# Opening of an attention and Fourier-mixing kernel: heads' table on 128-row diagonals, four full products a query tile, and a new order of sums and scalings

## The chip, the cores and the metric

The kernel runs on one core of one Trainium2 chip. The metric is the device time of one execution in microseconds; the time before is the median of three runs. A profiled execution has a span of its own, from the first to the last instruction of the record, and the text keeps the two apart. Engines are named as the profile names them: PE is TensorE (PEld its weight loads), DVE is VectorE, ACT is ScalarE, POOL is GpSimd, SP is the queue that issues most DMAs.

## The reference

Efficient attention (two softmaxes and two small products), then a Fourier mixing layer with a layer norm and a feed-forward block. B = 8 batches, 8 heads of 64, S = 576 tokens, D = 512, all float32.

```python
q_s = softmax(q, axis=-1)                     # over the 64 columns of a head, + 1e-9 in the sum
k_s = softmax(k, axis=2)                      # over the 576 tokens, + 1e-9 in the sum
kv  = einsum('bhsd,bhse->bhde', k_s, v)       # one 64x64 table a head
x   = einsum('bhsd,bhde->bhse', q_s, kv)      # heads side by side: x is (B, 576, 512)
mixed = real(fft(fft(x, axis=1), axis=2))
u   = x + mixed
un  = (u - mean(u)) / sqrt(var(u) + 1e-6)     # over the 512 columns
out = u + maximum(un @ w_ch1, 0) @ w_ch2      # 512 -> 2048 -> 512
```

## The kernel before

All eight batches go through the same stages. Batch 0 is done alone in a hand-ordered opening, while the weights' first chunks load and are converted; from the first feed-forward products of batch 0 (`half`, L1467) a long script interleaves the feed-forward of one batch with the attention and mixing of the next.

**Order.** Steps are closures with a time. `opening` builds the steps of batch 0 and gives them names; the string `OPENING` lists name and time, and `WARM` lists filler products (`warm`, L270) whose results nobody reads. All steps of the kernel are sorted by that time, and each engine runs its own instructions in that order. The time is a sort key only; what an instruction waits for follows from the data and from the buffers.

**The opening, in the order of the data.** `first_keys` takes the keys of four head pairs (k00 to k03: 128 rows, two heads of 64, by 576 tokens): maximum on VectorE ("max", L554), exponential with its sum on ScalarE ("exp", L557), four transposes on TensorE ("turn", L562) and a copy out of PSUM on ScalarE ("four", L565). The fifth chunk of 64 tokens of all four is transposed together ("last", L570) and copied by VectorE ("fifth", L573). "inverse" (L576, L577) makes the reciprocals of the sums. "kv" (L586) multiplies keys and values into one PSUM tile, [128, 4, 64]: row 64h + d of pair r is row d of the table of head 2r + h. "scale" (L589) multiplies it by the reciprocals into `pairs[0]`, [128, 4, 65], whose 65th column holds ones and so gives the row sums of the queries.

The queries of batch 0 come as four tiles of 128 tokens: A (c = 0, u = 0), B (1, 1), C (0, 1), D (1, 0), and the shared tile t with the tokens that the folds treat apart. `q_exp_spread` is maximum (L968, VectorE), subtraction ("less", L973, GpSimd for A, B, C, VectorE for D and t) and exponential (L977, ScalarE). `q_turn` and `t_turn` transpose (L985) and copy (L996, L1006, ScalarE). The tile t is divided by its sums first (`q_inverse`, L946 to L957) and folded on GpSimd (`t_fold`, L1018 to L1026).

`own_times_kv` multiplies a tile by the table through `by_head` (L840): 4 pairs x 2 heads x 2 halves of the tokens, 16 products of 64 rows by 64 columns by 65, each on a quarter of the TensorE array. The profile counts two records of each float32 product, so 32. "inverse" (L862, L864) takes the reciprocal of the 65th column, "out" (L876) scales all 512 columns on VectorE; the same function can do it with eight activations on ScalarE, which `BY_ACT` chooses by tile. `t_times_kv` does the shared tile in the same way (L840 and L1061), ScalarE copies the results ("t parts", L1070 and L1073), and "t folds" (L1085 to L1088) folds them on VectorE.

`folded` adds and subtracts tokens: "tokens0" and "tokens2" are the sum and the difference of A and C, "tokens1" and "tokens3" those of D and B (L1104). "columns", "by" and "again" (L1110 to L1130) fold further, all on VectorE in batch 0. `blocks` holds the Fourier products: "e0" and "e1" (L1217) read the sums after "columns0" and "columns1", "e2" and "e3" (L1224) the differences, "tails" (L1234) reads the shared tile's folds. "z" and "y" copy the results out (L1246 to L1250; z2 and z3 on VectorE, the rest on ScalarE). `mix_own` (m0, m1: L1264 to L1295) transforms the columns, `norm` (L1321 to L1374) normalises and transposes for the feed-forward.

**Other work in these queues.** "roots" (L669) makes ScalarE load the table with the square root. "c0", "c1" and "c2" convert the first three chunks of weights (L391 to L399: two activations on ScalarE, two operations on VectorE, one addition on GpSimd). "kept0" (L632) keeps a copy of x of tile A in PSUM.

**Buffers.** PSUM tiles come from rings: `turned` (tag "tr", 2 buffers of one bank) and `two` (3 buffers of two banks). `flat` is `turned` seen as 512 columns. A new user of a buffer waits until the readers of the last one are done. `halves` gives the 512-column working tiles of the folds (6 buffers), the tag "root" a single small one.

## Time and profile before

| | |
|---|---|
| runs | 1005.66, 1006.8, 1005.86 us; median 1005.86 us |
| profiled execution, span | 1006.6 us |
| TensorE busy | 995.6 us, 99% |
| VectorE, ScalarE, GpSimd busy | 718.6, 493.2, 442.9 us |
| granted TensorE clock | full in each of the 40 slices |
| chain that ended last | PE 87%, DVE 7%, ACT 3%, DMA 1%, issue 1% |
| DMA | 236.37 MB, mean 235 GB/s |

The profile shows one execution. Rows of a timeline or of a chain have the start in us, the length in us, the engine, the line of the code and what is written and read; in brackets stands the idle time of the engine just before, and what ended it. "issue" is time in which the engine waited for nothing that the profile shows. Rows of the waits have the total in us, the number and the longest. A window row has, for a stretch, the busy time and the number of instructions of each engine, the granted clock (1.00 is full speed), the mean busy share of the DMA engines and their GB/s. Ends of matmuls are modelled, and starts of neighbours are the safer measure.

### The profile page before, as it was taken

To read this page: it belongs to the slowest core of one execution; us is meant where nothing else is said; L and a number is where in the kernel's file an instruction comes from. 1 tells how busy PE (TensorE), PEld (TensorE's weight loads), DVE (VectorE), ACT (ScalarE), POOL (GpSimd) and SP (SyncE) were. 2 spreads that over 40 slices of the span, in tenths; PEclk is the share of its full clock that TensorE was granted. 3 is DMA by queue.
4 is the path that set the end of the run, shared out by engine and by line. 5 is a ranking of instruction groups with operands and counts; after the bars stand their busy time and mean duration, and the time that the engine had idled before them with its cause. 6 is when DMAs were issued, how large, how long until landed. Compare 5 with 4: busy or idle time off the path is not lost.

```text
span 1006.6 us, 19808 instructions
## 1 busy us (share of the span) xinstructions
PE 995.6 (99%) x7562; PEld 855.7 (85%) x7562; DVE 718.6 (71%) x1356; ACT 493.2 (49%) x1277; POOL 442.9 (44%) x445
## 2 busy tenths in 40 slices
PE   8999999999999999999999999999999999999998
PEld 6844464888888899889988998899889998998897
DVE  6898898666765887588756877688667945685563
ACT  4585642872468228832775177625772342151200
POOL 4263420357535637664655465655646450040000
PEclk9999999999999999999999999999999999999999
DMA  9987499687989666975677577847753765674573
GB/s 300 258 281 245 158 240 346 205 243 226 342 283 272 230 230 219 266 237 210 251 220 242 206 269 237 253 174 270 231 204 135 267 213 200 224 265 172 183 256 132
DMA packets 123559, 236.37 MB, mean 235 GB/s; under 512 B 24184, under 2 KB 88440, under 8 KB 112840
## 3 DMA queue, kind: packets, MB, share of 16 engines
q1 hardware_dynamic: 123096, 234.58, 71.0%
q8 instruction: 60, 0.98, 0.4%
q14 instruction: 35, 0.29, 0.1%
q10 hardware_dynamic: 288, 0.26, 0.1%
q0 software_dynamic: 80, 0.26, 0.1%
HBM read 199.94 MB, written 39.06 MB: 237 GB/s over the span
## 4 chain that ended last, share of the span: by engine, by line
PE 87%; DVE 7%; ACT 3%; DMA 1%; issue 1%; SPq 0%; POOL 0%; DVEq 0%; POOLq 0%
PE bb L1544 16%; PE ba L1544 11%; PE bc L1544 11%; PE bb L1671 10%; PE ba L1671 7%; PE bc L1671 7%; PE bb L1641 5%; PE bc L1479 2%; PE bb L1760 2%; PE two L840 2%; PE one L755 2%; PE two L1207 1%; PE two L1264 1%; PE ba L1479 1%; PE bc L1760 1%; PE ba L1760 1%
## 5 line engine op out<-in xcount | busy, mean ns | idle before, releaser
L1544 PE MATMUL bb<-unT,big 128*128 128x256 f32 x768 | 183.3, 380 | 0.0
L1544 PEld LDWEIGHTS bb<-unT,big 128*128 128x128 f32 x768 | 144.8, 190 | 20.7 <-DVE u L1514 0.7
L1556 ACT ACTIVATE big<-big 128x512 f32<-128x512 f32 x96 | 59.8, 629 | 147.6 <-DVE big L1555 141.0
L1544 PE MATMUL ba<-unT,big 128*128 128x256 f32 x512 | 123.9, 382 | 0.0
L1544 PE MATMUL bc<-unT,big 128*128 128x256 f32 x512 | 121.5, 380 | 0.1
L817 ACT ACTIVATE qT<-q 32x128 f32<-32x128 f32 x384 | 117.9, 307 | 5.9 <-DVE q L807 0.8
L1544 PEld LDWEIGHTS bc<-unT,big 128*128 128x128 f32 x512 | 96.9, 190 | 13.7 <-DVE big L1555 0.5
L1544 PEld LDWEIGHTS ba<-unT,big 128*128 128x128 f32 x512 | 95.5, 190 | 13.9 <-issue 0.5
L1514 DVE TENSOR_TENSOR u<-bb,s 128x512 f32<-128x512 f32 x66 | 45.2, 685 | 85.0 <-PE bb L1544 66.5
L1671 PE MATMUL bb<-big 128*128 128x128 f32 x848 | 103.8, 276 | 0.2 <-DVE u L1678 0.2
L1671 PEld LDWEIGHTS bb<-big 128*128 128x128 f32 x848 | 98.9, 192 | 1.0 <-DVE u L1678 1.0
L1390 POOL COPY unT<-unT 32x256 f32<-32x256 f32 x98 | 42.0, 428 | 90.2 <-DVE unT L1382 85.9
L1621 POOL TENSOR_TENSOR x<-x,big 128x512 f32<-128x512 f32 x45 | 60.9, 1368 | 46.0 <-DVE big L1678 19.7
L1617 DVE TENSOR_TENSOR big<-big 128x512 f32<-128x512 f32 x98 | 79.9, 842 | 0.0
L1671 PE MATMUL ba<-big 128*128 128x128 f32 x640 | 79.0, 276 | 0.0
L1671 PEld LDWEIGHTS ba<-big 128*128 128x128 f32 x640 | 75.0, 192 | 0.8
L1390 ACT COPY unT<-unT 32x256 f32<-32x256 f32 x126 | 50.7, 402 | 31.3 <-DVE unT L1382 29.5
L804 POOL TENSOR_TENSOR q<-q,qm 128x512 f32<-128x512 f32 x24 | 25.8, 1073 | 88.2 <-DVE qm L799 53.1
L405 POOL TENSOR_TENSOR big<-big 128x512 f32<-128x512 f32 x24 | 30.4, 1268 | 68.4 <-ACT big L1556 68.4
L1641 PE MATMUL bb<-big 128*128 128x256 f32 x256 | 58.3, 379 | 0.0
L1555 DVE TENSOR_TENSOR big<-bc,u 128x512 f32<-128x512 f32 x64 | 44.0, 688 | 17.3 <-PE bc L1544 16.4
L1641 PEld LDWEIGHTS bb<-big 128*128 128x128 f32 x256 | 48.0, 190 | 6.1
(336 smaller groups left out, 1917.9 us busy)
## 6 DMA issues: line engine op xcount, KB each, us to landing
big<-w2d SPq DMA_DIRECT2D x67, 1024.0 KB, 4.6
big<-w1s SPq DMA_DIRECT2D x64, 896.0 KB, 4.7
big<-w2s SPq DMA_DIRECT2D x16, 1024.0 KB, 4.8
big<-in_w_dram SPq DMA_DIRECT2D x21, 512.0 KB, 6.0
w2d<-big SPq DMA_DIRECT2D x42, 256.0 KB, 6.5
kb<-in_kT_dram SPq DMA_DIRECT2D x28, 320.0 KB, 7.8
q<-in_q_dram SPq DMA_DIRECT2D x28, 256.0 KB, 6.0
vt<-in_v_dram SPq DMA_DIRECT2D x84, 80.0 KB, 2.7
```

Source lines behind the costliest of these rows:

```text
L405: e1.tensor_tensor(out=to(4), in0=at(2), in1=at(3), op=ALU.add)
L817: nc.scalar.activation(to[t, i * Q:i * Q + Q], one, ACT.Exp)
L1390: copy(to, of)
L1514: plus = lambda t: V.tensor_tensor(out=temp(t), in0=box["bb"][:], in1=box["s1"][:], op=ALU.add)
L1544: nc.tensor.matmul(bank()[:, i, :], lhsT=w[:, WA_AT[m], k * P:(k + 1) * P], rhs=self.unT[g][:, B_AT[m], k, :], start=first and i == 0 and ...
L1555: steps = [(0, lambda: V.tensor_tensor(out=hp(i), in0=bank()[:], in1=u()[:], op=ALU.add)), (0.8, lambda: nc.scalar.activation(hp(i), hp(i) ...
L1556: (0.8, lambda: nc.scalar.activation(hp(i), hp(i), ACT.Relu))]
L1617: e.tensor_tensor(out=to(o), in0=to(x), in1=to(y), op=op)
L1621: E.tensor_tensor(out=x, in0=x, in1=tile(m), op=ALU.add)
L1641: nc.tensor.matmul(box[name][:, i, :], lhsT=h[p][:, A_AT[m], i * P:(i + 1) * P], rhs=self.stream[n][:, p, :], start=p == 0 and (m != 1 or ...
L1671: nc.tensor.matmul(box[place[n]][:, i, :], lhsT=own(m)(A_AT[n])[:, f, :], rhs=w[:, r // 2, r % 2 * P:r % 2 * P + P], start=first and f == ...
L1760: nc.tensor.matmul(bank()[:, i, :], lhsT=h[p][:, A_AT[m], i * P:(i + 1) * P], rhs=w[:, p, :], start=first and i == 0 and p == 0, stop=p == ...
```

## The change

The heads' table of batch 0 moves from `pairs[0]` to a new tile `diagonal`, [128, 4, 2, 65], in a part of the weights' space that is still free. For pair r it holds 130 columns: head 2r in the upper 64 rows and the first 65 columns, head 2r + 1 in the lower 64 rows and the last 65, zeros elsewhere. The ones and zeros of the sum columns are set by four memsets on GpSimd; "inverse" multiplies them by the reciprocals (`both`), and "scale" multiplies the products by `both`, so that the zeros come out of the same operation. A query tile then needs four products of the full array, 128 rows by 128 tokens by 130 columns, instead of 16 (`first_times_kv`). The shared tile takes four products of 128 columns and four of 64 tokens by 128 columns, in two tiles of the "tr" ring (`first_t_times_kv`).

Moved between engines: the copy "fifth" from VectorE to ScalarE; "out" of tile B from VectorE to eight activations on ScalarE; "tokens2" from VectorE to GpSimd, behind a one-column copy (`gate`) that reads what "columns0" writes.

Moved in the order: "k0 inverse" ahead of A's maximum; C's and D's maxima behind B's; the turns of C, t and D behind the products of keys and values; "tokens0" and "columns0" between the scalings of C and B; "e0" ahead of the shared tile's product, "e1" behind it; "t folds" behind all other folds.

```diff
-8.90 A max, 9.50 B max, 9.58 k02 four, 9.65 A less, 9.77 k0 last, 10.10 k0 inverse, 10.27 k03 turn, 10.42 k0 fifth,
-10.69 B less, 10.80 A exp, 11.30 k03 four, 11.84 B exp, 11.85 A turn, 12.20 C max, 12.45 A copy, 12.80 D max, 12.90 C less,
-12.95 B turn, 13.00 t max, 13.10 D less, 13.20 t less, 13.55 B copy, 14.00 k00 kv, 14.01 k01 kv, 14.10 C exp, 14.11 C turn,
-14.12 D exp, 14.13 t exp, 14.14 C copy, 14.2 k02 kv, 14.3 k03 kv, 14.4 D turn, 14.41 D copy, 14.75 t inverse, 14.76 k0 scale,
-14.8 t normal, 15.0 A kv, 15.1 t turn, 15.31 t copy, 15.4 C kv, 15.45 B kv,
-18.48 A inverse, 18.50 A out, 18.60 C inverse, 18.61 C out, 18.62 D kv, 18.90 B inverse, 19.01 B out, 19.63 D inverse,
-19.70 D out, 20.00 t fold, 20.1 t join, 20.2 t kv, 20.3 t parts, 20.43 tokens0, 20.5 columns0, 20.6 e0,
-20.70 tokens1, 20.80 columns1, 20.9 e1, 21.02 roots,
...
-21.15 t folds, 21.2 tokens2, 21.3 tokens3, 21.35 columns2, ...
+8.84 k0 inverse, 8.90 A max, 9.50 B max, 9.58 k02 four, 9.65 A less, 9.77 k0 last, 10.27 k03 turn, 10.3 k0 fifth, 10.32 k03 four,
+10.43 C max, 10.69 B less, 10.80 A exp, 10.9 D max, 11.80 C less, 11.84 B exp, 11.85 A turn, 12.20 t max, 12.25 D less,
+12.4 t less, 12.45 A copy, 12.46 C exp, 12.47 D exp, 12.5 t exp, 12.95 B turn, 13.4 B copy,
+14.00 k00 kv, 14.01 k01 kv, 14.2 k02 kv, 14.3 k03 kv, 14.31 C turn, 14.32 C copy, 14.4 t inverse, 14.5 k0 scale, 14.6 t normal,
+15.0 A kv, 15.1 C kv, 15.15 t turn, 15.16 t copy, 15.2 D turn, 15.3 D copy, 15.45 B kv, 15.5 D kv, 15.6 t fold, 15.7 t join,
+18.48 A inverse, 18.50 A out, 18.60 C inverse, 18.61 C out, 18.7 tokens0, 18.75 columns0, 18.90 B inverse, 19.01 B out,
+19.25 tokens2, 19.4 D inverse, 19.45 D out, 19.5 tokens1, 19.55 columns1, 19.6 tokens3,
+20.2 e0, 20.3 t kv, 20.4 t parts, 20.9 e1, 21.02 roots,
...
+21.35 columns2, ... 21.85 e3, 21.89 t folds, 21.9 tails,
...
-BY_ACT, BY_DVE = "", (2, 3)
+BY_ACT, BY_DVE = "B", (2, 3)
...
+        self.diagonal = self.w1sb[:, 8:10, :].rearrange("p a n -> p (a n)")[:, 0:NR * n].rearrange("p (r h n) -> p r h n", r=NR, h=2)
+                nc.gpsimd.memset(self.diagonal[64 * i:64 * i + 64, :, h, DH:], float(h == i))
...
         def fifth():
-            copy(self.fifth[64:], box["last"][64:])
+            nc.scalar.copy(self.fifth[64:], box["last"][64:])
...
             V.reciprocal(rec[:], rec[:])
+            V.tensor_tensor(out=both[:], in0=self.diagonal[:, :, :, DH], in1=rec[:].unsqueeze(2).to_broadcast([P, NR, 2]), op=ALU.mult)
...
         def scale():
-            V.tensor_tensor(out=self.pairs[b][:, :, 0:DH], in0=box["kv"][:, :, 0:DH],
-                            in1=rec[:].unsqueeze(2).to_broadcast([P, NR, DH]), op=ALU.mult)
+            V.tensor_tensor(out=self.diagonal[:, :, :, 0:DH], in0=box["kv"][:, :, 0:DH].unsqueeze(2).to_broadcast([P, NR, 2, DH]),
+                            in1=both[:].unsqueeze(3).to_broadcast([P, NR, 2, DH]), op=ALU.mult)
...
+    def first_times_kv(self, it, act=False):
+        def times():
+            q, px = self.live.pop(it)[0], self.two()
+            for r in range(NR):
+                nc.tensor.matmul(px[:, r // 2, r % 2 * 2 * n:(r % 2 + 1) * 2 * n], lhsT=q[:, r, :],
+                                 rhs=self.diagonal[:, r].rearrange("p h n -> p (h n)"), start=True, stop=True)
...
+                        nc.scalar.activation(x[:, a, k, :], px[:, a, k, 0:DH], ACT.Copy, scale=rec[:, a, k:k + 1])
...
+    def first_t_times_kv(self):
+        def times():
+            px = [self.flat() for _ in range(2)]
+            for r in range(NR):
+                nc.tensor.matmul(px[0][:, r * P:(r + 1) * P], lhsT=self.F[:, 2 * r, 0:P], rhs=table(r), start=True, stop=True)
+            for a in range(2):
+                for i in range(2):
+                    nc.tensor.matmul(px[1][64 * i:64 * i + 64, a * P:(a + 1) * P], lhsT=self.F[:, 2 * (2 * i + a), P:], rhs=table(2 * i + a),
+                                     start=True, stop=True)
...
+            nc.scalar.copy(g[:, 0:D], box[0])
+            for i in range(2):
+                nc.scalar.copy(x[:, i * HD:(i + 1) * HD], box[1][64 * i:64 * i + 64, 0:HD])
...
+                e, op = ((V if b < 2 else G), ALU.add) if i < 2 else (G if (b, i) == (0, 2) else V, ALU.subtract)
                 eo[i] = self.halves()
+                if (b, i) == (0, 2):
+                    gate = self.small.tile([P, 1], F32, tag="root", name="gate", bufs=1)
+                    G.tensor_copy(gate[:], eo[0][:, 1:2])
```

The folds of "t folds" become a function of their own (`g_folds`) with the same three operations; nothing else of the kernel changes.

65 lines of the change are left out of this document (46 added, 19 removed).

## The prediction

> **What bounds the kernel now.** I read the page first, then the waits of TensorE over the whole run, then the chain of waits cut to the opening, then the timeline of the opening engine by engine. The change touches only the opening, so the first question is whether microseconds won there reach the end.
>
> ```profile
> span 1006.6 us, 19808 instructions
> ...
> PE 995.6 (99%) x7562; PEld 855.7 (85%) x7562; DVE 718.6 (71%) x1356; ACT 493.2 (49%) x1277; POOL 442.9 (44%) x445
> ```
>
> ```profile
> PE two L840 <- issue: 1.5, 1, 1.5
> ...
> PE ba L1467 <- ACT eo L1326: 0.9, 1, 0.9
> PE tr L985 <- DVE q L957: 0.5, 1, 0.5
> ```
>
> TensorE is busy 99% of the span, and its two longest waits on work lie in the opening: the stall of 1.5 and the 0.9 before the first feed-forward products (L1467). From those on no wait is over 0.5, so they start the rest of the kernel: what the opening wins there is kept one for one, if the conversions of the weights, which also begin then, move with it. The opening itself is bound thus:
>
> ```profile
> 9.94 1.28 DVE qm L968 x2
> ...
> 20.22 1.52 issue
> ...
> 33.32 0.43 DVE Z L1246
> ...
> 36.40 4.33 PE tr L270 x20
> ```
>
> These rows of the chain (start, length, what) say: once the queries have landed, VectorE works through the maxima and on to the scaled heads' table, the query tiles are multiplied by it, VectorE divides and folds, TensorE transforms, the transforms are copied (33.32), and m0, m1, the filler products of L270 and the layer norm follow. The 1.52 us of "issue" is a stall of TensorE in the middle of a query tile, with no semaphore behind it.
>
> **The change part by part.** First the time to the table, from the timeline (start, duration, engine, line, shapes, idle time before).
>
> ```profile
> 9.29 0.19 ACT L557 ACTIVATION_READ_ACCUMULATOR big<-big,km 128x1 f32 x1
> ...
> 9.94 1.28 DVE L968 TENSOR_REDUCE qm<-big 128x8 f32<-128x512 f32 x2 [1.48 <-DMA big<-in_q_dram]
> ...
> 10.71 2.04 POOL L973 TENSOR_TENSOR big<-big,qm 128x512 f32<-128x512 f32 x2 [5.44 <-DVE qm L968]
> ...
> 13.51 1.04 POOL L973 TENSOR_TENSOR big<-big,qm 128x512 f32<-128x512 f32 x1 [0.76 <-DVE qm L968]
> ...
> 14.71 1.78 ACT L977 ACTIVATE big<-big 128x512 f32<-128x512 f32 x3
> ...
> 16.52 0.69 DVE L946 TENSOR_REDUCE qrec<-big 128x8 f32<-128x512 f32 x1 [0.70 <-ACT big L977]
> ...
> 17.68 0.42 DVE L589 TENSOR_TENSOR pairs<-two,kinv 128x256 f32<-128x256 f32 x1
> ...
> 18.92 0.17 DVE L862 TENSOR_SCALAR qrec<-two 128x8 f32<-128x8 f32 x1 [0.22 <-PE two L840]
> ...
> 19.36 0.69 DVE L876 TENSOR_TENSOR x<-two,qrec 128x512 f32<-128x512 f32 x1
> ```
>
> "k0 inverse", with its new product of 8 columns, moves ahead of A's maximum. Its sums are read by 9.48 (9.29 + 0.19); three small operations at the 0.2 us of the L862 row end at 10.1, so A's maximum starts 0.17 later than 9.94. The fifth chunk's copy leaves VectorE, and C's maximum follows B's at once, so GpSimd takes C's subtraction right behind B's: it ends near 13.9 (10.88 + 2.04 + 1.0) instead of 14.55. ScalarE starts B's exponential at 12.95, copies A, starts C's at 14.1 and ends C, D and t near 15.9 (14.1 + 1.78) instead of 16.49: 0.6 us earlier, and t's sum with it. The table is wider: 512 outputs, which I price by L876 (0.69, also from PSUM with a broadcast factor) and not by the 0.42 of L589. It starts at 17.08 (17.68 - 0.6) and ends at 17.77, against 18.10; the first product can start at 17.8 against 18.16. **Gain so far 0.33.** The wide table's extra 0.27 is in it; the bounds are the two rows. GpSimd's four small fills at the start lie in its 5.44 us of idle time.
>
> Next the products: two windows (busy time and records of TensorE, its loads, VectorE, ScalarE, GpSimd; granted clock, DMA share, GB/s), the queues from 19 to 21 us, and TensorE's timeline.
>
> ```profile
> 10.00:15.00 5.00, 4.96 (x54) 3.99 (x56) 4.90 (x9) 3.00 (x6) 3.47 (x7) 1.00 0.89 279
> 15.00:20.00 5.00, 4.79 (x140) 4.00 (x137) 3.91 (x10) 3.06 (x6) 0.27 (x1) 1.00 1.01 356
> ```
>
> ```profile
> q8 instruction: 1, 0.02, 2.8%
> ```
>
> ```profile
> 18.16 0.70 PE L840 MATMUL two<-pairs,big 64*64 64x65 f32 x32 [0.21 <-DVE pairs L589]
> 18.80 0.64 PE L985 MATMUL tr<-ident,big 128*128 128x128 f32 x4
> ...
> 21.74 1.04 PE L840 MATMUL two<-pairs,big 64*64 64x65 f32 x55 [1.52 <-issue]
> 22.72 1.56 PE L270 MATMUL tr<-pairs 128*128 128x256 f32 x6
> ...
> 24.73 0.41 PE L1061 MATMUL two<-pairs,F 64*64 64x64 f32 x16
> 25.57 1.71 PE L1217 MATMUL two<-ft,eo 128*128 128x144 f32 x12 [0.43 <-PE two L1061]
> 27.12 0.66 PE L1217 MATMUL two<-big,eo 128*128 128x144 f32 x4
> 27.61 0.91 PE L1217 MATMUL two<-ft,eo 128*128 128x144 f32 x4
> ...
> 31.32 1.22 PE L1224 MATMUL two<-ft,eo 128*128 128x144 f32 x8 [0.34 <-DVE eo L1130]
> 32.47 1.00 PE L1234 MATMUL two<-ft,eo 17*128 17x145 f32 x20
> ```
>
> From 19 to 21 us one packet passes on the instruction queue while the data queues are full (share 1.01), and TensorE resumes at 21.74, after 194 records in 10 us (54 + 140): I read the stall as TensorE out of fetched instructions. The change leaves 8 records a tile instead of 32, and 16 instead of 48 for the shared product: 128 fewer. The count reached at 20 us is then reached only in the shared product, about 27 us, long after the packet, so I take **1.5 us of stall away**. But the records get longer. One of 128x144 takes 0.122 (27.12 to 27.61 for four), so one of 130 columns about 0.11 and a tile 0.88, against 0.64 for 32 packed records (18.16 to 18.80): 0.24 a tile, 0.96 for four. The bounds are 0.11, by the row of the same full array, and 0.16, a tile at twice the packed one's time (2 x 0.64 / 8). I take the lower.
>
> From 17.8: A and C 1.76, the turns of t and D 0.86, B 0.88, to 21.3. D's product waits for D's copy on ScalarE, behind t's: t's turn ends at 20.25, two copies of 0.58 end at 21.47. D's product ends at 22.4, where the filler L270 stood at 22.72. So the stall's 1.5 is mostly paid back: to the longer records, and to the turns moved into this stretch. **Gain 0.35.**
>
> [...]
>
> Then VectorE, from one row of its timeline and, for what moves to GpSimd and ScalarE, two of the groups kept apart by shape.
>
> ```profile
> 22.38 0.17 DVE L862 TENSOR_SCALAR qrec<-two 128x8 f32<-128x8 f32 x1 [1.11 <-PE two L840]
> ```
>
> ```profile
> L1104 POOL TENSOR_TENSOR eo<-x 128x512 f32<-128x512 f32 x12 | 16.7, 1396 | 0.0
> ```
>
> ```profile
> L927 ACT ACTIVATE q<-q,qm 128x64 f32<-128x64 f32 x24 | 6.4, 336 | 1.5 <-DVE qm L921 1.5
> ```
>
> It loses B's scaling and the fifth copy (both near 0.69) and one difference of tokens (to GpSimd); A's and C's scaling end as before (21.27 = 22.38 - 1.11) and are followed at once by tokens0 where it used to idle for 1.11. It would be through with everything, shared folds last, near 29.5 instead of 31.7. GpSimd's difference, which its new one-column copy holds back until columns0 is through, starts after the join near 24.1, where only conversions after 30 us queue behind it; at 1.4 (L1104) it ends by 25.5, before the folds that read it, and TensorE needs those only at 30. B's eight scalings on ScalarE, 64 columns each, take from 22.8 between 0.6 (one L1070 copy of all 512) and 2.1 (8 x 6.4 / 24 by L927); I take 1.1, and TensorE reads what they lead to (e1) only at 27.4. All this is cover, no gain, because TensorE now has more in front: filler 1.3 (to 23.7), e0 of 20 records 2.45 (26.1), shared product, 8 records of 0.109 and 8 half-wide ones at half or the whole of that (27.4 to 27.85), e1 2.45 (to 30.3), L1224's step 1.15, tails 0.85: **the transforms are ready at 31.8 to 32.3, against 33.32.** TensorE alone would gain 1.0 to 1.5.
>
> Last, what is queued behind the shared product, which moved behind e0.
>
> ```profile
> 25.20 0.58 ACT L1070 COPY eo<-two 128x512 f32<-128x512 f32 x1 [5.14 <-PE two L1061]
> 25.69 0.74 ACT L1073 COPY xs<-two 64x256 f32<-64x256 f32 x2
> 26.45 1.28 ACT L669 ACT_TABLE_LOAD   x1
> ...
> 30.15 0.58 ACT L632 COPY two<-x 128x512 f32<-128x512 f32 x1
> 33.53 0.65 ACT L1246 COPY Z<-two 128x256 f32<-128x256 f32 x2 [2.80 <-PE two L1234]
> ...
> 34.78 0.36 ACT L1273 COPY sn<-tr 128x256 f32<-128x256 f32 x1
> ```
>
> ScalarE copies the shared product, loads the square root's table, starts four conversions, keeps x (ending 30.73), then waits 2.80 for z1 and z0. The product's last result came at 25.14; now it comes at 27.6 to 28.0, and its copies end at 28.5 to 28.8 instead of 26.43: 2.1 to 2.4 later. The rest keeps its 4.30 us (26.43 to 30.73), so ScalarE is free at 32.8 to 33.1. That is after the tails and only 0.4 to 0.7 before the old 33.53. **ScalarE takes over as the bound.** What follows needs both engines: z1 and z0 feed m0's last products, and the sn copy ends 1.61 after z1's start (34.78 + 0.36 - 33.53). Between ScalarE's 0.4 to 0.7 and TensorE's 1.0 to 1.5 I take 0.75, near ScalarE's end. The filler of 4.33 (L270) follows m1 as before, so turns, norm and first products move by the same.
>
> Sum: 1006.6 - 0.75 = 1005.85 for this profiled execution. It stands 0.7 above the median of the three runs, 1005.86, so the runs' time is 1005.1.
>
> **The rivals.** *TensorE alone decides* (1.0 to 1.5): if the shared copies can begin with the first half of the product and the column halves overlap fully, ScalarE is free at 32.5 or before. For it: the product's two halves have PSUM tiles of their own. Against: the two last copies need the second one. Time 1005.86 - 1.25 = 1004.6.
>
> *VectorE's whole gain arrives* (2.2 at its last fold, and a little where a later wait that is just met drops out). For it: the chain before shows VectorE between the products and L1246. Against: TensorE's own sum above. Time 1005.86 - 2.36 = 1003.5.
>
> *Slower: the full products cost what packing had saved.* Between the table and ScalarE's last shared copy lie 48 records (four tiles, shared product). Each 0.01 us more a record delays that copy by 0.48, and ScalarE has 0.75 to lose: slower begins at 0.125 a record; at 0.16 the copy is (0.16 - 0.109) x 48 = 2.45 later, so 1.7 slower: 1007.6. [...] Against: full records of L1217 at 0.122 for 144 columns, loads included.
>
> *The stall stays*: fetched instructions are late again, at the same count, now inside the shared product. For it: the queues' share of 1.01. Against: 7 us more for the packet to come. The price is 1.5 on ScalarE's chain: 0.75 slower, 1006.6.
>
> **How the numbers follow.** Forecast (ScalarE bounds) 0.46, TensorE alone 0.20, VectorE's whole gain 0.18, costlier products 0.11, the stall stays 0.05. This kernel's measurement tells about 0.2%, 2.0 us, from no change. Faster by more: VectorE's case and a fifth of TensorE's, 0.22. Slower by more needs 0.166 a record and up ((2.0 + 0.75) / 48 more); I give that 0.08 of the 0.11. Within: 0.70. The forecast's own range is 1004.5 to 1005.6. The range for 8 in 10 reaches to VectorE's case and to the stalled one and just beyond: 1003.2 to 1006.9.
>
> **What would show it.** Right: L840's rows gone, full products of about 0.9 a tile with no "issue" gap inside; the scaled table starting near 17.1 and lasting 0.7; the shared copies near 27.5; ScalarE without idle time before z1, and z1 near 32.9; the filler of L270 ahead of the turns starting near 35.5 instead of 36.24. Wrong: a tile of 1.2 or more, an idle ScalarE before z1 (TensorE's case), or a first feed-forward product that does not move while the filler does (the norm would then hold it). If that product moves but the end does not, the weights' conversions gave the gain back.

## The result, and the profile after

| | before | after |
|---|---|---|
| median, runs (lowest to highest) | 1006.80 us, 15 runs (1005.65 to 1009.86) | 1009.24 us, 15 runs (1008.26 to 1011.97) |
| profiled execution, span | 1006.6 us | 1007.3 us (its run: 1009.12 us) |

The ratio is 1.0026, with a 95% interval of 1.0018 to 1.0034: the change made the kernel 2.6 us slower (1.8 to 3.4). Forecast was 0.75 faster.

The page of after:

```profile
span 1007.3 us, 19569 instructions
...
PE 996.3 (99%) x7434; PEld 857.9 (85%) x7434; DVE 719.9 (71%) x1354; ACT 495.6 (49%) x1286; POOL 444.9 (44%) x451
```

TensorE has the 128 records fewer that were counted (7562 to 7434), is busy 0.7 us longer, and is still busy 99% of the span. So the opening is again the place to look. Its timeline in after, all engines (start, length, engine, line, shapes, idle time before and what ended it):

```profile
9.78 0.18 DVE L583 RECIPROCAL kinv<-kinv 128x4 f32<-128x4 f32 x1
11.44 0.17 DVE L584 TENSOR_TENSOR krec<-big,kinv 128x8 f32<-128x8 f32 x1 [1.48 <-DMA big<-in_q_dram]
11.53 2.58 DVE L1033 TENSOR_REDUCE qm<-big 128x8 f32<-128x512 f32 x4
...
18.29 0.69 DVE L596 TENSOR_TENSOR big<-two,krec 128x512 f32<-128x512 f32 x1
...
19.04 2.06 PE L865 MATMUL two<-big 128*128 128x130 f32 x16 [0.20 <-DVE big L596]
...
22.43 0.95 DVE L1173 TENSOR_TENSOR eo<-x 128x512 f32<-128x512 f32 x1
...
22.80 0.85 POOL L1086 TENSOR_TENSOR T<-F 128x120 f32<-128x120 f32 x1
...
24.67 1.75 ACT L882 ACTIVATE x<-two,qrec 128x64 f32<-128x64 f32 x8 [2.02 <-DVE qrec L871]
...
26.45 0.69 DVE L1173 TENSOR_TENSOR eo<-x 128x512 f32<-128x512 f32 x1 [0.88 <-ACT x L882]
27.15 1.27 POOL L1173 TENSOR_TENSOR eo<-x 128x512 f32<-128x512 f32 x1
27.18 1.39 DVE L1184 TENSOR_TENSOR eo<-eo 128x128 f32<-128x128 f32 x1
...
33.21 1.00 PE L1303 MATMUL two<-ft,eo 17*128 17x145 f32 x20 [0.35 <-ACT big L402]
...
33.55 0.61 ACT L639 COPY two<-x 128x512 f32<-128x512 f32 x1
...
34.25 0.65 ACT L1315 COPY Z<-two 128x256 f32<-128x256 f32 x2
...
34.71 1.11 DVE L396 TENSOR_SCALAR big<-big 128x512 int32<-128x512 int32 x1
...
36.47 0.75 DVE L1350 TENSOR_TENSOR eo<-tr,sn 128x256 f32<-128x256 f32 x2
```

Four things stand in it. The new product of 8 columns (L584) waits 1.48 us for a DMA, and A's maximum (L1033) behind it starts at 11.53 where it started at 9.94 before. Two tiles of full products take 2.06 us, with no gap inside (L865). VectorE waits 0.88 for the eight scalings on ScalarE (L882), and its next fold of 128 columns (L1184) takes 1.39 while GpSimd works on tokens2. At 34.71 a conversion of weights on VectorE (L396) takes 1.11; its second step (L399, 0.69) and then m0's sums stand behind it. The first feed-forward product, from TensorE's timeline, comes 1.06 later than the 42.70 of before:

```profile
43.76 1.53 PE L1536 MATMUL ba<-unT,big 128*128 128x256 f32 x6 [0.88 <-ACT eo L1395]
```

### The profile page after: what moved, and what is told of

Read it like the earlier page. It is cut to its first block, busy times and chain, and to the rows that moved or that the text cites. A ratio compares the mean times of both kernels' runs of the same rounds, so it can differ in the third digit from the quotient of the medians.

```text
span 1007.3 us, 19569 instructions
## 1 busy us (share of the span) xinstructions
PE 996.3 (99%) x7434; PEld 857.9 (85%) x7434; DVE 719.9 (71%) x1354; ACT 495.6 (49%) x1286; POOL 444.9 (44%) x451
## 4 chain that ended last, share of the span: by engine, by line
PE 84%; DVE 7%; DMA 2%; ACT 2%; SPq 2%; issue 1%; POOL 1%; POOLq 0%; DVEq 0%
PE bb L1613 16%; PE ba L1613 11%; PE bc L1613 10%; PE bb L1740 10%; PE ba L1740 7%; PE bc L1740 7%; PE bb L1710 5%; PE bc L1548 2%; PE two L847 2%; PE one L762 2%; PE two L1276 1%; PE bb L1829 1%; PE ba L1548 1%; PE ba L1829 1%; PE two L1333 1%; PE bb L1548 1%
```

## A table to read the experiments by

All kernels below were compared with the kernel before on the same chip. Times of stages are starts in us in the one profiled execution of each; "A to FF" is from A's maximum to the first feed-forward product, "stall" the length of the "issue" gaps of TensorE in the opening. From m0's sums to that product it is 7.28 to 7.31 in all of them.

| kernel | A's max. | table | tails | z1 | m0 sums | FF | A to FF | stall | ratio (95%) |
|---|---|---|---|---|---|---|---|---|---|
| before | 9.94 | 17.68 | 32.47 | 33.53 | 35.40 | 42.70 | 32.76 | 1.52 | 1 |
| e4 (before) | 10.24 | 17.98 | 32.41 | 33.47 | 35.33 | 42.63 | 32.39 | 1.17 | one run |
| e12 (before) | 10.20 | 17.93 | 31.98 | 33.03 | 34.90 | 42.20 | 32.00 | 0.76 | 1.0002 [0.9993, 1.0011] |
| after | 11.53 | 18.29 | 33.21 | 34.25 | 36.47 | 43.76 | 32.23 | none | 1.0026 [1.0018, 1.0034] |
| e1 | 9.98 | 16.83 | 31.70 | 32.74 | 34.96 | 42.26 | 32.28 | none | 1.0012 [1.0003, 1.0021] |
| e2 | 10.12 | 16.97 | 32.35 | 33.41 | 35.27 | 42.57 | 32.45 | none | 1.0015 [1.0006, 1.0024] |
| e3 | 10.24 | 16.95 | 31.18 | 32.22 | 34.45 | 41.73 | 31.49 | 0.50 | 1.0000 [0.9991, 1.0009] |
| e5 | 10.47 | 18.20 | 32.87 | 33.93 | 35.79 | 43.10 | 32.63 | none | 1.0005 [0.9996, 1.0014] |
| e6 | 9.72 | 16.56 | 30.91 | 32.41 | 34.27 | 41.57 | 31.85 | none | 1.0002 [0.9993, 1.0011] |
| e7 | 9.79 | 16.57 | 30.71 | 31.76 | 33.63 | 40.93 | 31.14 | 1.01 | 1.0000 [0.9991, 1.0009] |
| e8 | 9.80 | 17.61 | 31.99 | 33.05 | 34.91 | 42.22 | 32.42 | none | 1.0003 [0.9994, 1.0012] |
| e9 | 9.88 | 17.85 | 38.86 | 39.91 | 41.78 | 49.08 | 39.20 | 4.69 | 1.0080 [1.0067, 1.0094] |
| e10 | 10.28 | 17.74 | 31.39 | 32.44 | 34.50 | 41.79 | 31.51 | 0.83 | 1.0001 [0.9992, 1.0010] |
| e11 | 10.11 | 17.22 | 31.66 | 33.10 | 35.02 | 42.32 | 32.21 | none | 1.0008 [0.9999, 1.0017] |

A's maximum starts when its queries have landed, anywhere from 9.7 to 10.5, so lengths from there on are the better measure. In the three executions of the kernel before, "A to FF" less the stall is 32.76 - 1.52 = 31.24, 32.39 - 1.17 = 31.22 and 32.00 - 0.76 = 31.24: **31.23 us of work, and a stall of varying length.**

## The experiments

### e1: the product of 8 columns after the maxima

```diff
         def inverse():
             ...
-            V.tensor_tensor(out=both[:], in0=self.diagonal[:, :, :, DH], in1=rec[:].unsqueeze(2).to_broadcast([P, NR, 2]), op=ALU.mult)
+        def mask():
+            V.tensor_tensor(out=both[:], in0=self.diagonal[:, :, :, DH], in1=rec[:].unsqueeze(2).to_broadcast([P, NR, 2]), op=ALU.mult)
-12.25 D less, 12.4 t less
+12.25 D less, 12.3 k0 mask, 12.4 t less
```

> Edit: of the changed kernel, the product of the reciprocals with the ones and zeros of the new table is taken out of k0 inverse, ahead of A's maximum, and done between the subtractions of D and t. Theory (a wait that only the memory region makes): in the changed kernel this product started at 11.44 us, 1.48 later than it could, when the last rows of the shared tile had landed, and A's maximum behind it at 11.53 instead of 10.1; without it A's maximum starts within 0.2 of 10.1, the scaled table starts 1.0 to 1.5 earlier than 18.29, the first feed-forward product 1.0 to 1.5 earlier than 43.76, and the median falls by as much, to 0.9998 to 1.001 of the kernel before. Rival (the landing of the queries, which fell late in that profile, held A's maximum): A's maximum starts near 11.4 again and nothing moves by over 0.4. Rival (what costs lies behind the table: longer products, ScalarE's queue, GpSimd beside VectorE): the table starts earlier but the first feed-forward product moves by less than 0.5.

Median 1008.15 us, ratio 1.0012. The timeline of e1, all engines:

```profile
9.98 2.60 DVE L1035 TENSOR_REDUCE qm<-big 128x8 f32<-128x512 f32 x4 [0.26 <-DMA big<-in_q_dram]
...
16.83 0.64 DVE L598 TENSOR_TENSOR big<-two,krec 128x512 f32<-128x512 f32 x1
...
25.64 1.26 POOL L1175 TENSOR_TENSOR eo<-x 128x512 f32<-128x512 f32 x1
25.67 1.38 DVE L1186 TENSOR_TENSOR eo<-eo 128x128 f32<-128x128 f32 x1
...
31.26 0.29 DVE L1119 TENSOR_TENSOR eo<-eo 128x128 f32<-128x128 f32 x1
31.47 0.42 DVE L396 TENSOR_SCALAR big<-big 128x512 int32<-128x512 int32 x1
...
31.70 1.00 PE L1305 MATMUL two<-ft,eo 17*128 17x145 f32 x20 [0.35 <-ACT big L402]
...
32.07 0.57 ACT L641 COPY two<-x 128x512 f32<-128x512 f32 x1
32.53 0.75 DVE L1317 COPY Z<-two 128x256 f32<-128x256 f32 x2
...
32.74 0.65 ACT L1317 COPY Z<-two 128x256 f32<-128x256 f32 x2
32.75 1.28 POOL L404 TENSOR_TENSOR big<-big 128x512 int32<-128x512 int32 x1 [5.85 <-ACT two L641]
...
33.20 1.12 DVE L396 TENSOR_SCALAR big<-big 128x512 int32<-128x512 int32 x1
...
34.11 0.39 PE L1338 MATMUL tr<-cd,Zr 128*128 128x129 f32 x2
...
34.35 0.69 DVE L399 SCALAR_TENSOR_TENSOR big<-big 128x512 int32<-128x512 int32 x1
...
34.96 0.75 DVE L1352 TENSOR_TENSOR eo<-tr,sn 128x256 f32<-128x256 f32 x2
```

A's maximum starts 1.55 earlier than in after, and the table 1.46, the tails 1.51, z1 1.51, m0's sums 1.51 and the first feed-forward product 1.50 earlier: the wait passes through the whole opening undiminished. On the clock 1.0026 became 1.0012, 1.4 us by the ratios and 1.1 by the medians: that much was expected, but the ratio stayed just above the expected 0.9998 to 1.001. The product doesn't need the queries. It reads the sum columns of `diagonal`, and that tile lies in the weights' space, the "big" of the rows; the awaited transfer is the shared tile's first rows, which line 304 writes to every 32nd partition of another part of that space. The view of that line in after has:

```profile
L304 SPq DMA_DIRECT2D big<-in_q_dram x1: 695/695/695, 8.5 to 8.5; - x1
...
  DVE krec L584: 1.5, 1
```

The last line says that L584 waited 1.5 us for it; by its semaphore the transfer landed at 11.32. A read of 8 columns was made to wait for a strided write it has nothing to do with. Not every read of the space waits so: in e1 the same transfer landed at 11.09, and A's maximum, which also reads "big", had begun at 9.98. What makes the one wait and not the other, the stride or something else, no run here shows.

### e2: the shared product ahead of e0

```diff
 (e1, and)
-20.2 e0, 20.3 t kv, 20.4 t parts, 20.9 e1
+20.1 t kv, 20.15 t parts, 20.2 e0, 20.9 e1
```

> Edit: as the first run, and the shared tile's product and its copies stand ahead of e0 again. Theory of the prediction (ScalarE's queue behind the shared product bounds the transforms' copies once the early wait is gone): the shared copies start 2.0 to 2.5 earlier, ScalarE gets an idle time before z1 of over 1 us, and z1 comes 0.3 to 0.8 earlier than in the first run; the median falls by as much. Rival (TensorE or VectorE bounds there): z1 moves by less than 0.2, or TensorE waits for the shared tile's folding on GpSimd and everything comes later by up to 1 us.

Median 1008.49 us, ratio 1.0015. The timeline of e2, all engines:

```profile
24.57 1.16 PE L898 MATMUL tr<-big,F 128*128 128x128 f32 x8 [0.79 <-POOL F L1093]
...
33.41 0.65 ACT L1317 COPY Z<-two 128x256 f32<-128x256 f32 x2 [2.02 <-PE two L1305]
```

ScalarE now idles 2.02 before z1, so its queue no longer sets z1; yet z1 comes 0.67 later than in e1, where 0.3 to 0.8 earlier was expected. TensorE waits 0.79 for GpSimd's join (L1093) in front of the shared product, and hands that on. In the profiles the order with e0 first is the better of the two, by 0.17 in "A to FF"; the ratios of 1.0012 and 1.0015 don't separate them. Taking the load off ScalarE in this way gains nothing. In e1 VectorE's copy of the transforms starts at 32.53 and z1 0.21 later, just as far behind it as in before (33.32 and 33.53), although ScalarE comes to z1 without idle time: its queue is one of several chains that end together there.

### e3: the new order with the packed products

The kernel before, with the new order as in e2, the fifth copy and B's scaling on ScalarE, and tokens2 with its `gate` on GpSimd; the table stays in `pairs[0]`, all products stay packed.

```diff
 (before, and)
-OPENING = ... (order of before)
+OPENING = ... (order of after, t kv and t parts ahead of e0)
-            copy(self.fifth[64:], box["last"][64:])
+            nc.scalar.copy(self.fifth[64:], box["last"][64:])
-                e, op = ((V if b < 2 else G), ALU.add) if i < 2 else (V, ALU.subtract)
+                e, op = ((V if b < 2 else G), ALU.add) if i < 2 else (G if (b, i) == (0, 2) else V, ALU.subtract)
+                if (b, i) == (0, 2): ... G.tensor_copy(gate[:], eo[0][:, 1:2])
```

> Edit: the kernel before, with its 64-row table and its 16 packed products a tile, but with the order of the changed kernel (the shared product ahead of e0, since its PSUM buffer is taken from another ring), the fifth copy and B's scaling on ScalarE and the difference of tokens on GpSimd. It has no product with ones and zeros, so no early wait. Theory (the wait explains the loss, the full products are worth their price): it lies within 0.2% of the kernel before, with an issue stall of over 1 us inside the packed products, and is not faster than the second run by more than 0.5 us. Rival (the full products cost what packing had saved): it is faster than the second run by 1 us or more. Rival (the new order costs, GpSimd's difference beside VectorE): it is slower than the kernel before by 1 us or more.

Median 1007.14 us, ratio 1.0000. Against e2, which differs in the products and their table alone, it is 1.35 us less by the medians, and "A to FF" is 31.49 with a stall of 0.50 in it, against 32.45. So the first rival held (1 us or more), and not the theory: the full products cost this order more than the stall that they remove.

### e4 and e12: the kernel before, run again

> The kernel before as it is, for a second profile. Theory: its span is 1004.5 to 1005.6, below the 1006.6 of the first profile, since fifteen runs of it have a median of 1006.8 and a run lies some 1.75 above its span; the queries land within 0.5 of 9.92, and an issue stall inside the packed products shows again, of 1 to 2 us. Rival (the first profile was typical): 1006.4 or more. If the stall is under 0.5 here, the gain that was expected from its removal was not there to take in most executions.

> The kernel before against itself, for the size of the noise and a third profile. Theory: ratio within 0.9994 to 1.0006; the profile has an issue stall of 1.0 to 1.6 us in the packed products. If the profiled execution is again 1 us or more above the median of its own runs, and the wide ones (five of five below theirs) are not, profiled executions of the packed kernel are longer than timed ones.

One run of 1008.22 us for e4. For e12 a median of 1007.13 and a ratio of 1.0002 [0.9993, 1.0011]: a ratio within 0.0009 of 1 can't be told from no change here. Two expectations failed: e4's span was 1006.4, so the first profile was no exception, and e12's stall was shorter than the 1.0 expected. TensorE's timelines of e4 and of e12 have the stall at the same record as the profile of before, 55 records from the end of B's and D's products, at other times and lengths:

```profile
21.68 1.04 PE L840 MATMUL two<-pairs,big 64*64 64x65 f32 x55 [1.17 <-issue]
```

```profile
21.24 1.04 PE L840 MATMUL two<-pairs,big 64*64 64x65 f32 x55 [0.76 <-issue]
```

### e5: filler products where the stall comes

```diff
 (before, and)
-(10.5, 5, 256, 1), (18.63, 3, 256)
+(10.5, 5, 256, 1), (15.43, 3, 256), (18.63, 3, 256)
```

Three products of 256 columns, read by nobody, between C's and B's products.

> Edit: the kernel before, with three more filler products of 256 columns (1.3 us of TensorE, results read by nobody) between C's and B's products, where the profiles of the kernel before show the issue stall of 1.2 to 1.5 us. Theory (the stall is of the profiled execution; the executions that are timed have it not, or much shorter: the two profiled executions of the kernel before took 1008.37 and 1008.22, its 27 runs have a median of 1006.9): in the profile the filler lies in the stall's place and the first feed-forward product moves by less than 0.5, but the median rises by 0.6 to 1.4 us, since B's and D's products now really come later. Rival (the stall is in every execution): neither the profile nor the median moves by over 0.4.

Median 1007.81 us, ratio 1.0005 [0.9996, 1.0014]. TensorE's timeline of e5:

```profile
20.52 1.56 PE L270 MATMUL tr<-pairs 128*128 128x256 f32 x6
22.01 1.16 PE L840 MATMUL two<-pairs,big 64*64 64x65 f32 x64
```

1.5 us of work went in and no gap is left in the 64 records behind it; "A to FF" became 32.63, 0.63 more than in e12, 0.24 more than in e4 and 0.13 less than in the profile of before. In the profile, filler took the place of stall. The timed difference of 0.5 lies within 0.9 either way, so it doesn't tell a stall of one microsecond from none: inconclusive by itself.

### e9: a burst of short products

```diff
 (before, and)
+        placed.append((15.43, lambda: self.burst(64)))
+    def burst(self, n):
+        t, some = [self.flat(), self.flat()], self.pairs[1][:].rearrange("p r n -> p (r n)")
+        for j in range(n):
+            a, c = slice(64 * (j // 2 % 2), 64 * (j // 2 % 2) + 64), slice(64 * (j % 2), 64 * (j % 2) + 64)
+            self.nc.tensor.matmul(t[j // 2 % 2][c, 0:65], lhsT=some[a, 0:64], rhs=some[a, 0:65], start=True, stop=True)
```

64 packed products (128 records) read by nobody, between C's and B's.

> Edit: the kernel before, with 64 more packed filler products (64 rows by 64 by 65 columns, 128 records, some 2.2 us of TensorE, results read by nobody) between C's and B's products. They use up half a kilobyte-block's worth of instructions each way: the count at which the stall of the kernel before falls comes inside them, and the next one, 256 records and loads later, near D's products, where the packet of the second block has not come (it came at 25.6 in both profiles). Theory (TensorE runs out of fetched instructions in every execution): the profile shows a second issue stall of 2 to 4 us near 24, the first feed-forward product comes 4 to 6 us later than 42.65, and the median rises by 3.5 to 6 us. Rival (such stalls are of the profiled execution): the profile as above, but the median rises by 1 to 2.5 us, the time of the added products. Rival (the stall has nothing to do with the number of instructions): no second stall, the profile and the median rise by 1 to 2.5 us.

Median 1015.02 us (5 runs, 1014.20 to 1015.89), ratio 1.0080. TensorE's timeline of e9:

```profile
20.06 0.56 PE L277 MATMUL tr<-pairs 64*64 64x65 f32 x9
21.20 1.92 PE L277 MATMUL tr<-pairs 64*64 64x65 f32 x116 [0.59 <-issue]
22.91 0.22 PE L848 MATMUL two<-pairs,big 64*64 64x65 f32 x1
22.95 0.23 PE L277 MATMUL tr<-pairs 64*64 64x65 f32 x3
22.97 0.33 PE L848 MATMUL two<-pairs,big 64*64 64x65 f32 x8
27.40 1.46 PE L848 MATMUL two<-pairs,big 64*64 64x65 f32 x55 [4.10 <-issue]
```

The first stall stands again 9 records behind C's products, though the records are others. The second comes exactly 116 + 1 + 3 + 8 = 128 records later; each record has its weight load (the page of before counts 7562 of each), so that is 256 instructions. The window of the last 2.4 us before TensorE resumes (busy time and instructions of PE, PEld, VectorE, ScalarE, GpSimd; clock, DMA share, GB/s) and the packets of the instruction queue from 23.0 to 27.4 us (packets, MB, share):

```profile
25.00:27.40 2.40, 0.00 (x0) 0.00 (x0) 0.00 (x0) 0.00 (x0) 0.00 (x0) 1.00 1.06 372
```

```profile
q8 instruction: 1, 0.02, 1.3%
```

No engine does anything while the data queues run full, and one packet of instructions goes through in 4.4 us. It is of 16 KB and passes from 24.99 to 25.93, 1.47 before TensorE resumes. The same holds for all eight stalls of before, e3, e4, e7, e9, e10 and e12: a packet of 16 KB on that queue ends 1.4 to 1.6 before TensorE resumes, and the next one starts 3.7 to 3.9 after. I read these rows so: TensorE is starved of instructions, the two times of e9 a block of 256 apart, and a fetch takes some 6.2 us here (21.20 to 27.40): 3.8 until the packet starts, 0.9 for the packet and 1.5 until TensorE runs. How many instructions TensorE holds ahead of its work, no run here shows.

And the stall is no artefact of the profile: the median rose 8.0 us (6.7 to 9.5), so the rival of 1 to 2.5 falls, and so does the theory's own size, 3.5 to 6. "A to FF" rose by 7.97 against the 31.23 without stall (39.20 - 31.23) and by 6.4 to 7.2 against the three profiles of before with theirs; the interval holds the first and part of the second, and doesn't tell whether the median of before has a stall.

### e6 and e11: the work back on VectorE

```diff
 (e1, and for e6)
-BY_ACT, BY_DVE = "B", (2, 3)
+BY_ACT, BY_DVE = "", (2, 3)
 (for e6 and for e11)
-                e, op = ... (G if (b, i) == (0, 2) else V, ALU.subtract)
+                e, op = ... (V, ALU.subtract)
-                if (b, i) == (0, 2): ... G.tensor_copy(gate[:], eo[0][:, 1:2])
-19.25 tokens2, 19.4 D inverse, 19.45 D out, 19.5 tokens1, 19.55 columns1, 19.6 tokens3
+19.4 D inverse, 19.45 D out, 19.5 tokens1, 19.55 columns1, 19.58 tokens2, 19.6 tokens3
```

> Edit: as the first run (the changed kernel without the early wait), with B's scaling and the difference of tokens back on VectorE, and no gate on GpSimd. Theory (VectorE had to wait 0.88 for B's scaling on ScalarE, and its folds of 128 columns took 1.38 and 0.55 beside GpSimd's operations instead of 0.29): tokens1 starts within 0.3 of the first run's 24.94, its columns take 0.3 each, and e1 comes no later; the shared folds end within 0.5 of the first run; the median moves by less than 0.5 either way. Rival (the offload is a gain as meant, 1.3 us of VectorE): slower by 0.8 or more. Rival (the offload costs what it saves and more): faster by 0.8 or more.

> Edit: as the first run (the changed kernel without the early wait), with only the difference of tokens back on VectorE and no gate on GpSimd; B's scaling stays on ScalarE. Theory (of the 1.0 us that both moves cost, GpSimd's part is the fold of 1.38 instead of 0.29, ScalarE's the wait of 0.88): half of it comes back; the fold of 128 columns behind tokens1 takes 0.3, VectorE still waits 0.7 to 0.9 for B's scaling, the tails start 0.2 to 0.6 earlier than 31.70, the median 0.2 to 0.8 us below the first run. Rival (only the waiting for ScalarE costs): within 0.2 of the first run. Rival (only GpSimd costs): all of it, 0.8 to 1.2 us.

e6: median 1007.48 us, ratio 1.0002. e11: median 1007.55, ratio 1.0008. The timeline of e6, all engines:

```profile
24.62 0.69 DVE L1172 TENSOR_TENSOR eo<-x 128x512 f32<-128x512 f32 x1
...
25.35 0.29 DVE L1183 TENSOR_TENSOR eo<-eo 128x128 f32<-128x128 f32 x1
...
31.76 0.76 DVE L1314 COPY Z<-two 128x256 f32<-128x256 f32 x2
...
32.04 1.30 POOL L404 TENSOR_TENSOR big<-big 128x512 int32<-128x512 int32 x1 [7.18 <-ACT big L403]
...
32.41 0.65 ACT L1314 COPY Z<-two 128x256 f32<-128x256 f32 x2
32.43 1.20 DVE L396 TENSOR_SCALAR big<-big 128x512 int32<-128x512 int32 x1
```

The fold of 128 columns that took 1.38 in e1 takes 0.29 when GpSimd is idle. In e1 GpSimd's subtraction starts at 25.64 and VectorE's fold at 25.67, and VectorE ends only 0.15 after GpSimd: its fold is 1.09 longer than in e6, beside a subtraction of 1.26. Not all work of VectorE is held up so: in e6 its scaling out of PSUM (L886) at 22.86 takes 0.69 beside GpSimd's L1092 (22.85, 0.66 long), as in before at 19.36 with GpSimd idle (there L876). Why the one is longer and the other is not, no run here shows. So moving 0.69 of VectorE's work to GpSimd cost VectorE 1.09. B's scaling cost VectorE a wait of 0.88 for the 0.69 it gave up:

```profile
25.39 0.69 DVE L1172 TENSOR_TENSOR eo<-x 128x512 f32<-128x512 f32 x1 [0.88 <-ACT x L884]
...
26.11 0.29 DVE L1183 TENSOR_TENSOR eo<-eo 128x128 f32<-128x128 f32 x1
```

This is e11's timeline: the fold is short again, the wait is still there. "A to FF" is 32.28 in e1, 32.21 in e11 and 31.85 in e6, so by these single profiles the two moves cost the opening 0.43 together, nearly all of it by B's scaling. On the clock, 1.0012 to 1.0002 points the same way, but two intervals of 0.0009 don't prove it; and e11's tails came only 0.04 earlier than e1's, where 0.2 to 0.6 was expected.

Two more things stand in these traces. In e6 VectorE copies its transforms at 31.76, but ScalarE, without idle time before it, reaches z1 only at 32.41, 0.65 later instead of 0.21: with the two moves undone, ScalarE's queue is the bound there that the prediction took it for. And tokens0 and columns0, which the new order puts beside GpSimd's fold of the shared tile, take 0.95, 0.38 and 0.54 in e6 (in e1 0.95, 0.38 and 0.55), for 0.68, 0.29 and 0.28 in before and in e8, where they come after that fold: 0.6 us that e6 didn't win back. GpSimd's own fold L1088 takes 0.85 there for 0.40.

### e7 and e10: packed products without the moves

e7 is e3 with the same undoing as e6; e10 is e7 with C's turn back among the products of keys and values and D's right behind them, ahead of A's product:

```diff
 (e7, and)
-14.2 k02 kv, 14.3 k03 kv, 14.31 C turn, 14.32 C copy, ... 15.2 D turn, 15.3 D copy
+14.15 C turn, 14.16 C copy, 14.2 k02 kv, 14.3 k03 kv, 14.35 D turn, 14.36 D copy
```

> Edit: the kernel before with the changed order, as the third run (packed products, the fifth copy on ScalarE), with B's scaling and the difference of tokens on VectorE as before. Theory: the front of the new order brings the table 0.7 to 1.0 earlier (16.95 in the third run's profile), and nothing behind it costs any more, so the median is 0.3 to 1.0 below the kernel before, the first feed-forward product in the profile near 41.7. Rival (the third run's tie with the kernel before has another cause, later in the kernel): within 0.3 of the kernel before again.

> Edit: as the seventh run (packed products in the new order, all scalings and folds on VectorE), with C's turn between the products of keys and values as before, and D's ahead of A's product. Theory: D's product no longer waits for a copy behind t's, the first feed-forward product comes 0.2 to 0.8 earlier than 40.93, and the median is 0.3 to 1.2 us below the kernel before. Rival: the queues of TensorE and ScalarE ahead of the table are full, the table comes later by the turn's 0.4, nothing is won.

e7: median 1006.92 us, ratio 1.0000; e10: 1007.17, ratio 1.0001. Neither is the 0.3 or more below the kernel before that was expected, and e10's first feed-forward product came 0.86 later than e7's instead of earlier: both rivals held. e7 has the earliest first feed-forward product of all, 40.93, with a stall of 1.01 still in it. e10's table starts 1.17 later than e7's, of which A's maximum explains 0.49: the turns behind the products of keys and values are worth 0.68 there, and "A to FF" says 0.37 (31.51 against 31.14). None of it shows on the clock.

### e8: the wide table and the full products alone

The kernel before with `diagonal` and the full products, but its own order; the product of 8 columns stands ahead of the shared tile's sum, and nothing is moved between engines.

```diff
 (before, and the wide table and full products of after)
-14.75 t inverse, 14.76 k0 scale
+14.74 k0 mask, 14.75 t inverse, 14.76 k0 scale
```

> Edit: the kernel before with the wide table and the full products only, in the old order, nothing moved to ScalarE or GpSimd, the product with ones and zeros just ahead of t's sum, so that it waits for nothing. Theory (full products cost 1.0 to 1.4 us and take away a stall that timed executions do not have): in the profile no issue stall, the first feed-forward product within 0.6 of 42.65; the median 0.8 to 1.6 us above the kernel before. Rival (the stall is real in timed executions): the median within 0.5 of the kernel before or below it.

Median 1007.83 us, ratio 1.0003. TensorE's timeline of e8:

```profile
18.35 1.16 PE L867 MATMUL two<-big 128*128 128x130 f32 x8 [0.48 <-DVE big L598]
...
19.79 2.85 PE L867 MATMUL two<-big 128*128 128x130 f32 x24
```

Three tiles follow one another in 22.48 - 19.79 = 2.69 until the filler starts, 0.90 a tile and 0.112 a record; there is no gap. "A to FF" is 32.42, 1.19 above the 31.23 of the packed kernel without its stall. So the full products with their wider table and their wait for it cost 1.19, and the stall that goes with the packed ones was 0.76 to 1.52: the exchange is about even in the profiles. The timed ratio of 1.0003 agrees (0.8 to 1.6 us slower was expected), but its interval reaches to 1.2 us slower and doesn't prove it.

## Why the prediction was wrong, point by point

Forecast was 0.75 us faster, measured 2.6 slower. The steps that failed are the price of "k0 inverse", a base that stood 1.6 above the median, and VectorE's moves as cover.

- **What bounds the kernel**: right. What the opening lost reached the end (e1 against after, e9 against before). In the fourteen profiled executions the span less the start of the first feed-forward product is 963.1 to 964.2 us, while that start runs from 40.93 to 49.08.
- **"k0 inverse" ahead of A's maximum, three small operations that end at 10.1: the step that failed.** Two ended at 9.96; the third waited to 11.44. Its operation was priced, but the prediction didn't ask in which tile its inputs lie, nor which transfer into that tile was under way. Forecast price 0.17, measured 1.4 to 1.5, undone in e1.
- **The time to the table**: right once the wait is gone, 16.83 in e1 for 17.08; the wide scaling took 0.64 to 0.69 for 0.69.
- **The full products**: right, 0.90 a tile for 0.88. The rival that priced them at twice the packed time fell; it would have been 0.16 a record, and 0.112 was measured. So the rivals with the right sign, this one and the stall that stays, named other mechanisms: after has no "issue" gap in its products. No run shows the factor of two behind the 0.16: here a tile of packed products was 0.64 and a full one 0.90, 1.4 times.
- **The stall**: its cause was read rightly (e9), and the full products do remove it. Its size was taken from one execution, 1.52; two others have 1.17 and 0.76. How much of it the timed median pays was not asked.
- **VectorE's moves as cover, no gain and no cost**: wrong. VectorE was forecast to end its folds near 29.5 and ended them at 31.26 + 0.29 = 31.55 in e1, just ahead of the tails. B's scalings took 1.75, within the bounds of 0.6 to 2.1, yet VectorE stood behind them for 0.88; GpSimd's subtraction took 1.26 for 1.4, but VectorE stood behind that too, for 1.09; and its first folds lost 0.6 beside GpSimd's fold of the shared tile. Together that is 2.6, where VectorE had scaled A and C 0.4 earlier than forecast (20.89 for 21.27): 29.5 - 0.4 + 2.6 = 31.7, near the 31.55 measured. The price was looked for in TensorE's readers, and not in VectorE's own queue or in what GpSimd does beside it.
- **TensorE's order and ScalarE as the bound**: in e1 VectorE's copy of the first transforms starts at 32.53 (forecast: ready at 31.8 to 32.3). TensorE had stood 0.35 before the tails; the row names ScalarE's L402, whose result the tails don't read, and the last of what they do read is VectorE's fold that ends at 31.55. Then x is kept by 32.64 and z1 follows at 32.74 without idle time (forecast 32.8 to 33.1), and the filler ahead of the turns starts at 35.45 (forecast 35.5). So the steps held to within 0.3; that ScalarE alone decides did not in e1, and did in e6.
- **From z1 to the first product "by the same"**: short by 0.35. In e1 TensorE's part of m0 was ready as early as forecast, but VectorE was still in a conversion: L396 had taken 1.12 (from 33.20) for 0.42, beside GpSimd's addition of the chunk before (L404, 1.28 from 32.75), and L399 ran behind it. Before, VectorE copied z2 and z3 out of PSUM during that addition and did the conversion in 0.49. Before, the sums start 0.11 after the end of TensorE's last record for them (34.90 + 0.39 to 35.40); in e1 that would be 34.11 + 0.39 + 0.11 = 34.61, and they start at 34.96. The forecast 0.75 less 0.35 is 0.40, and e1's first product comes 0.44 ahead of the profile of before. This is read from rows of after, e1 and e6; no run tested it alone.
- **The base**: the profiled execution was said to stand 0.7 above the median of three runs. A run reads 1.8 above its span (1009.12 and 1007.3 in after), so it was a run of about 1008.4, 1.6 above the median of 15. The sum was made against an execution that was long, and that had the longest stall of the three.

What adds up: the wait is 11.53 less 10.1 (A's maximum in the three executions of before), 1.4 us; the rest of the change has an "A to FF" of 32.28 for 31.23 and a stall, so 1.05 dearer against a stall of 0.76 to 1.52. By the profiles that would make after 0.9 to 1.7 slower; the runs say 1.8 to 3.4. Against the one execution that the sum was made from, it closes: 0.75 forecast, less 0.35 for VectorE's conversions, is the 0.40 that e1 shows; that execution stood 1.6 above its median, and e1's profiled run (1007.96) within 0.2 of its own, so e1 is 1.2 slower by the medians; with the wait's 1.4 that is 2.6.

**What stays open** is that rest of about one microsecond, and it is the same in other kernels. e1 reaches the feed-forward when e12 does (42.26 and 42.20) and before the other two, and is timed 1.2 us slower; e6 reaches it 0.6 to 1.1 earlier, and is timed even. If the median execution of before had no stall, its "A to FF" would be 31.23, and e1, e2, e6, e8, e9, e11 would be 1.05, 1.22, 0.62, 1.19, 7.97 and 0.98 slower by the table; by their ratios they are 1.2, 1.5, 0.2, 0.3, 8.1 and 0.8 slower. That fits within the intervals, and so does the fact that the three profiled executions of before were runs of 1008.4, 1008.2 and 1007.9, all above its medians of 1006.8 to 1007.4. Against it: e7 with its stall of 1.01 stands at 31.14, level with 31.23, and is timed even, so it would have to pay a stall in the median that the kernel before, with nearly the same instructions, doesn't; and e5, 1.40 slower by the same count, is timed 0.5. Nothing here has measured the stall in an execution that wasn't profiled in full, so how much of it the median of before pays isn't settled. No version beat the kernel before by more than the comparison can tell.

## What to carry to other kernels

When an instruction is moved ahead in an engine's queue, list not only its operands but the tiles that hold them, and every transfer into those tiles that is still under way: not each of them holds a read, but one did here, for 1.48. Before moving VectorE's work to GpSimd or ScalarE, look whether VectorE reads the result soon or folds at the same time: here that cost it 0.88 and 1.09 for two operations of 0.69. A stall that belongs to no instruction should be seen in several executions before its length enters a sum.

## What was not expected of the hardware

- TensorE stopped with no semaphore behind it at a fixed place in the program (ahead of the 55 records of before, e4, e12 and e9) for a time that varies: 0.76 to 1.52 us, and 4.10 in e9, where the 128 records since the stop before, with their weight loads, had been worked off in 2.1 us (21.20 to about 23.3). It resumed 1.4 to 1.6 us after a 16 KB packet of instructions had passed.
- VectorE's operation on 128 columns went from 0.29 (e6, e11) to 1.39 us (after) beside one of GpSimd on 512 columns (1.27), and its conversion of 512 integers from 0.42 to 1.11 (after) and 1.20 (e6) beside GpSimd's addition (1.29 and 1.30).
- Eight activations of 128 rows by 64 columns from PSUM, each with a factor a row, took 1.75 us on ScalarE (L882 of after), 0.22 each, where VectorE scales all 512 columns in 0.69 (L876 of before).
